# Sequence 0's filter products with frequencies on the partitions

## The chip, the core and the metric

The kernel runs on one core of a Trainium2 chip. The metric is the device time of one execution in microseconds (us), as the median of several runs. The core has five engines with a queue each: PE (TensorE, with its weight loads shown apart as PEld), DVE (VectorE), ACT (ScalarE), POOL (GpSimd) and SP (which here only issues transfers). Transfers run on 16 DMA engines. SBUF holds tiles of up to 128 partitions, PSUM takes what PE makes, and DVE and ACT copy it out.

## What is computed

For each of 8 sequences of 3008 rows and 256 channels, a real Fourier transform along the rows, a product with a complex filter, and the transform back. Then an RMS norm and a gated FFN on each row:

```
X = rfft(x, axis=1)                       # x (8, 3008, 256): 1505 frequencies
y = irfft(X * (filt_r + 1j * filt_i), n=3008, axis=1)
t = y.reshape(24064, 256)
xn = t / sqrt(mean(t * t) + 1e-6) * rms_g
out = (silu(xn @ w_gate) * (xn @ w_val)) @ w_out     # 256 -> 1536 -> 256
```

The filters are two fp32 tables of 1505 x 256, 1.5 MB each. All inputs come in fp32; the matmuls of the kernel run in fp16.

## The kernel before

**The transform.** 3008 is 47 x 64. Stage A transforms along the 64 (matmul with `wa`), which leaves 32 groups `k2` (K2 = 32) of 96 rows (KR = 96: real and imaginary part of 48 values). Stage B is a matmul of each group with its own 96 x 96 table `wb[:, k2]`. Its result are the frequencies, 48 (SL) real and 48 imaginary, of which 24 ascend (k2 + 64 q) and 24 are mirrored (64 j - k2). They are multiplied with the filter. Stage Bi goes back with the tables `wi`, stage Ai with `wai`, and what comes out is `y` in the order that the norm wants.

**The FFN.** For each sequence there are 6 blocks of up to 512 rows, and 12 slices (`jt`) of the hidden width per block. One (sequence, block, slice) is a slot; there are 576. A slot's PE work is four matmuls of 512 columns (`gv`, L501, to `pg` and `pv`), and, two slots later, four of 256 columns (`down`, L526). ACT makes the silu (`sg`), DVE the product with `pv` (`hh`).

**The order.** It is written out by hand (`manual_schedule`). Each engine works its instructions off in the order of the program. While the FFN of one sequence runs, the mixing of the next is laid into its slots: a planner (`at`, `fit`, `a_plan`, `b_plan`, `norm_plan`) places units at slots so that two PSUM banks are not asked for twice and the estimated loads of ACT and DVE stay within a bound. The units are `a_unit` (stage A, one matmul of 512 columns and a copy), `z_store` and `t2_load` (a turn through DRAM), `b_unit` (four matmuls of 96 columns, `psb`), `s_part` and `add_unit` (the complex product with the filter `ff` and its sum), `yt_load` (a DMA transpose), `bi_unit`, `t4_load` (DMA transpose), `n_unit`, `sq_unit`, `stat_unit`, `xt_unit` and `tr_unit` (norm, and DMA transpose to `xn`).

**Sequence 0** has no FFN ahead of it to hide in, so it has a path of its own, the opening, with PE in place of the DMA turns:

1. `x_load` on POOL's queue, then `a0_unit` (L367) with short fills of PE (`fill`, L436).
2. `f_load`: the filter comes in six pieces, with 128 partitions of four whole rows each, on POOL's queue; `wb`, `wi` and two thirds of the FFN's weights (`w_load`) follow there.
3. `f_unit` (L399): the filter is turned by PE to channels on the partitions, and copied by ACT to `ff[128 channels, half, k2, 3 * 48]` (imaginary negated, imaginary, real). `f_neg` (POOL) makes the negated part, `f_last` one row.
4. `tr0_unit` (L377): the data are turned by PE to `t2`, 96 rows on the partitions.
5. For each of 16 units (four k2, one half of the channels): `b_unit` with the data as the stationary operand, so that channels are on the partitions of `psb`; two products on DVE, `s_part` (L238 with the real filter, L241 with the imaginary one and the two parts of `psb` swapped); `yt0_unit` (L428) adds the two and turns them back on PE, to 96 rows on the partitions; `bi_unit` (L292) does stage Bi.
6. `t4_first` (L444), `first_norm` (L456 to L480) for the first block, and `t4_load` by DMA for the others. Four `a_unit`s of sequence 1 and some fills stand between these steps.

Then the slots begin. `seen` (L681) is a tiny POOL copy that reads a transposed tile; what POOL issues after it waits for that tile.

Of the kernel before, what the change touches and what calls it, by code (L numbers as in the profile page):

```python
# [10 lines left out]
FP32 = mybir.dt.float32  # L11
# [27 lines left out]
def _make_tables():  # L39
# [58 lines left out]
    return tab, wb.astype(f), wi.astype(f)  # L98
# [3 lines left out]
def kernel(  # L102
# [13 lines left out]
    tab_np, wb_np, wi_np = _make_tables()  # L116
    tab_d = nc.inline_tensor(tab_np, name="tab_t").ap()
    wb_d = nc.inline_tensor(wb_np, name="wb_t").ap()
    wi_d = nc.inline_tensor(wi_np, name="wi_t").ap()

# [10 lines left out]
    sqp = ctx.enter_context(tc.tile_pool(name="sqp", bufs=2))  # L131
# [3 lines left out]
    hp = ctx.enter_context(tc.tile_pool(name="hp", bufs=4))  # L135
# [10 lines left out]
    wb = glob.tile([P, K2, KR], FP16)  # L146
# [4 lines left out]
    ff = glob.tile([P, 2, K2 + 1, 3 * SL], FP32)  # L151
# [37 lines left out]
    def bank(i, name):  # L189
        pool, tag = ((psM, "mx"), (psG, "pg"), (psV, "pv"), (psB, "mb"), (psO, "po0"))[i]  # L190
        return pool.tile([P, 512], FP32, tag=tag, name=name)
# [51 lines left out]
    def b_unit(b, i, bk=3, e=0):  # L243
        g, dh = divmod(i, 2)
        ps = bank(bk, "psb")[:, 0:4 * KR]
        for k in range(4):
            kk = 4 * g + k
            nc.tensor.matmul(ps[:, ts(k, KR)], st[b]["t2"][kk // KC][:, kk % KC, ds(dh * P, P)],  # L248
                             wb[0:KR, kk, :], start=True, stop=True)
# [4 lines left out]
    def b_soft(b, i, v=None):  # L254
        g, dh = divmod(i, 2)
        ps = bank(3, "psb")[:, 0:4 * KR]
        for k in range(4):
            kk = 4 * g + k
            nc.tensor.matmul(ps[:, ts(k, KR)], st[b]["t2"][kk // KC][:, kk % KC, ds(dh * P, P)],
                             wb[0:KR, kk, :], start=True, stop=True)  # L260
# [111 lines left out]
    def tr0_unit(g, eng):  # L372
        pool, tag = ((psO, "po0"), (psO, "po1"), (psM, "mx"))[g % 3]
# [9 lines left out]
    fst = {}  # L383
    FR4 = 4

    def f_load(i, f):
        if i not in fst:
            fst[i] = stg.tile([P, 2, FR4, D], FP32, tag="stg", name="fs")
        t = fst[i]
        row = FR4 * P * i if i < 2 else NF - 1 - FR4 * P  # L390
        for src in ((filt_i, filt_r)[f],):
            nc.gpsimd.dma_start(t[:, f].rearrange("p a d -> p (a d)"),
                                raw(src, row, [[FR4 * D, P], [1, FR4 * D]]))

    def f_unit(i, f, dh, e):
        t = fst[i]
        ps = bank(1 + "AV".index(e), "psf").rearrange("p (a q) -> p a q", a=FR4)
        for a in range(FR4):
            nc.tensor.transpose(ps[:, a, :], t[:, f, a, ds(dh * P, P)], idf)  # L399
        v = ps.rearrange("p a (q s) -> p s a q", s=16)  # L400
        fk = ff[:, dh, 0:K2].rearrange("p (t k) c -> p t k c", k=4)
        fu = ff[:, dh, 1:K2 + 1].rearrange("p (t k) c -> p t k c", k=4)[:, ::-1, ::-1, :]
        lo = SL * (1 + f) + 8 * i
        hi = lo + H
        if i < 2:
            copy(e, fk[:, :, :, lo:lo + 8], v[:, 0:8])
            copy(e, fu[:, :, :, hi:hi + 8], v[:, 8:16])
        else:
            copy(e, fk[:, :, :, lo:lo + 8], v[:, 8:16])
            copy(e, fu[:, :, :, hi:hi + 7], v[:, 0:8, :, 1:8])  # L410

    def f_last():
        v = ff.rearrange("p e k (s q) -> p e k s q", s=3)
        for dh in range(2):
            nc.gpsimd.tensor_copy(out=v[:, dh, 0, 1:3, H:SL - 1], in_=v[:, dh, K2, 1:3, H:SL - 1])
# [5 lines left out]

    def yt0_unit(i, eng, bk, ks=slice(0, 4)):
        g, dh = divmod(i, 2)
        s = st[0]["s"][i][1]
        ps = bank(bk, "psy")[0:KR].rearrange("p (k t) -> p k t", k=4)
        for k in range(4)[ks]:
            for e in range(2):
                nc.tensor.matmul(ps[:, k, :], s[e][:, k, :], ident, start=(e == 0), stop=(e == 1))  # L428
        if g not in st[0]["yt"]:
            yt_tile(0, g)  # L430
        copy(eng, st[0]["yt"][g][0:KR, ks, dh, :], ps[:, ks])
# [146 lines left out]
    with tc.manual_schedule():  # L578
# [49 lines left out]
        for u in todo[0:2]:  # L628
            f_unit(*u, "A")
# [240 lines left out]
```

## Time and profile before

| | |
|---|---|
| median of 3 runs | 859.22 us (858.91 to 859.23) |
| profiled execution | 859.02 us |
| its span | 857.2 us |
| PE, DVE, ACT, POOL busy in the span | 849.3, 556.1, 612.8, 300.4 us |
| first FFN matmul (`pg`, L501) in the chain of waits | 43.28 us |
| 16-unit product stage, DVE | 21.54 to 36.97 us |
| DMA moved | 108.24 MB |

The profile is of one execution of the program. Starts are counted from the start of the span. A line number can be that of a helper (`copy` is L195 on ACT and L197 on DVE). The span does not hold all of the execution's time: 1.8 us lie around it. PE records overlap, so a single matmul's duration is longer than its distance to the next.

### The profile page before, as it was taken

Reading aid. Unit: us, or ns where it says so; the run is one execution under the profiler, and the core shown is the slowest. Engines: PE = TensorE matmul, PEld = TensorE weight load, DVE = VectorE, ACT = ScalarE, POOL = GpSimd, SP = SyncE. Lnnn points to the kernel's source line nnn. Section 1 sums busy time; section 2 is a strip of 40 time slices with the busy share of each in tenths; the row PEclk is TensorE's granted clock in tenths of the full one; section 3 lists DMA queues with packets and bytes.
Section 4 is the critical chain, followed back from the end, with each engine's and each line's share of the span. In section 5 each row is a group of like instructions: output and inputs, shape, how many; then the busy total and the mean of one; then the engine's idle time right before and its main releaser. Section 6 shows DMA issues by size and latency. Waiting matters only on the chain.

```text
span 857.2 us, 16980 instructions
## 1 busy us (share of the span) xinstructions
PE 849.3 (99%) x6117; PEld 531.9 (62%) x6117; DVE 556.1 (65%) x922; ACT 612.8 (71%) x1343; POOL 300.4 (35%) x349
## 2 busy tenths in 40 slices
PE   8999999999999999999999999999999999999997
PEld 6756666666656666666666666666666666665654
DVE  5857655776666666666666676767666665555554
ACT  4986878786687757887578865887567765777444
POOL 5725732543154413443144430444123430132000
PEclk9999999999999999999999999999999999999999
DMA  9997698756976566747746648534554331521101
GB/s 284 271 182 151 148 191 162 148 124 143 186 137 133 117 134 119 158 113 129 157 126 110 130 99 172 119 77 117 129 115 93 99 72 41 125 52 50 63 25 50
DMA packets 199293, 108.24 MB, mean 126 GB/s; under 512 B 159622, under 2 KB 183576, under 8 KB 199208
## 3 DMA queue, kind: packets, MB, share of 16 engines
q1 hardware_dynamic: 190520, 85.78, 44.2%
q0 software_dynamic: 8544, 21.24, 12.8%
q8 instruction: 48, 0.79, 0.4%
q14 instruction: 37, 0.30, 0.1%
q10 hardware_dynamic: 144, 0.13, 0.0%
HBM read 45.78 MB, written 35.65 MB: 95 GB/s over the span
## 4 chain that ended last, share of the span: by engine, by line
PE 97%; DMA 1%; DVE 0%; ACT 0%; POOL 0%; issue 0%; POOLq 0%
PE po L526 29%; PE pv L501 28%; PE pg L501 28%; PE psb L248 3%; PE psi L292 3%; PE psn L321 2%; PE psa L204 2%; DMA fs<-in_filt_i_dram 1%; PE psy L428 1%; PE psf L399 1%; PE pst L377 0%; POOL xc L186 0%; DVE s L238 0%; ACT ff L195 0%; ACT sq L458 0%
## 5 line engine op out<-in xcount | busy, mean ns | idle before, releaser
L506 DVE TENSOR_TENSOR hh<-pv,sg 128x512 f16<-128x512 f32 (+1 forms) x577 | 391.5, 679 | 284.0 <-ACT sg L505 219.9
L505 ACT ACTIVATE sg<-pg 128x512 f16<-128x512 f32 (+1 forms) x577 | 337.5, 585 | 214.5 <-PE pg L501 210.7
L501 PE MATMUL pg<-xn,wg 128*128 128x512 f16 (+2 forms) x1156 | 337.9, 374 | 0.0
L501 PE MATMUL pv<-xn,wv 128*128 128x512 f16 (+2 forms) x1156 | 337.8, 374 | 0.0
L526 PE MATMUL po<-wo,hh 128*128 128x256 f16 x2256 | 332.6, 272 | 0.0
L526 PEld LDWEIGHTS <-hh 128*128 128x128 f16 x2256 | 213.5, 98 | 105.5
L275 POOL TENSOR_TENSOR ss<-s,s 128x384 f16<-128x384 f16 x112 | 101.9, 911 | 267.1 <-DVE s L241 239.5
L501 PEld LDWEIGHTS <-wv 128*128 128x128 f16 x1156 | 113.0, 98 | 130.6 <-issue 0.2
L501 PEld LDWEIGHTS <-wg 128*128 128x128 f16 x1156 | 111.6, 98 | 16.8 <-issue 0.2
L347 POOL TENSOR_TENSOR xt<-y,rho 128x1024 f16<-128x1024 f32 (+1 forms) x47 | 87.3, 1858 | 2.9
L329 ACT ACTIVATE junk<-y 128x256 f16<-128x256 f32 x184 | 76.0, 413 | 2.9
L241 DVE TENSOR_TENSOR s<-psb,ff 128x384 f16<-128x384 f32 x124 | 67.6, 547 | 0.3 <-POOL ff L419 0.3
L238 DVE TENSOR_TENSOR s<-psb,ff 128x384 f16<-128x384 f32 x124 | 67.6, 547 | 0.3 <-ACT ff L195 0.2
L195 ACT ACTIVATE uu<-psi 128x384 f16<-128x384 f32 (+1 forms) x127 | 61.8, 487 | 1.0
L195 ACT ACTIVATE y<-psn 128x512 f32<-128x512 f32 (+1 forms) x95 | 55.8, 588 | 4.4 <-PE psn L321 0.2
L292 PEld LDWEIGHTS <-yt 96*128 96x128 f16 x512 | 35.5, 97 | 26.2 <-issue 0.2
L339 POOL TENSOR_TENSOR rho<-u,mhalf 128x4 f32<-128x4 f32 (+1 forms) x47 | 47.6, 1012 | 3.9
L337 POOL TENSOR_SCALAR u<-ss 128x4 f32<-128x4 f32 (+1 forms) x47 | 9.1, 194 | 106.4 <-ACT junk L329 105.2
L292 PE MATMUL psi<-wi,yt 96*128 96x96 f16 x512 | 42.9, 205 | 0.0
L195 ACT ACTIVATE t<-psa 128x512 f16<-128x512 f32 x69 | 40.9, 594 | 2.4 <-PE psa L204 0.9
L248 PE MATMUL psb<-wb,t 96*128 96x96 f16 x480 | 40.0, 206 | 0.0
L248 PEld LDWEIGHTS <-t 96*128 96x128 f16 x480 | 29.3, 97 | 10.7 <-issue 0.2
(91 smaller groups left out, 361.0 us busy)
## 6 DMA issues: line engine op xcount, KB each, us to landing
out_dram<-o SPq DMA_DIRECT2D x40, 512.0 KB, 3.6
xc<-in_x_dram POOLq DMA_DIRECT2D x31, 384.0 KB, 5.7
z_tmp<-t SPq DMA_DIRECT2D x28, 384.0 KB, 2.6
t<-z_tmp SPq DMA_DIRECT2D x28, 384.0 KB, 6.0
out_dram<-o SPq DMA_DIRECT2D x7, 384.0 KB, 3.1
fs<-in_filt_i_dram POOLq DMA_DIRECT2D x3, 512.0 KB, 10.7
fs<-in_filt_r_dram POOLq DMA_DIRECT2D x3, 512.0 KB, 11.3
ws<-in_moe_w_gate_dram POOLq DMA_DIRECT2D x3, 512.0 KB, 10.0
```

What stands on the lines that cost most here:

```text
L195: nc.scalar.activation(out=out, in_=in_, func=AXT.Copy, **({} if scale is None else {"scale": scale}))
L238: eng.tensor_tensor(out=o, in0=ps, in1=f1, op=ALU.mult)
L241: eng.tensor_tensor(out=o, in0=ps[:, :, ::-1, :], in1=f2, op=ALU.mult)
L248: nc.tensor.matmul(ps[:, ts(k, KR)], st[b]["t2"][kk // KC][:, kk % KC, ds(dh * P, P)], wb[0:KR, kk, :], start=True, stop=True)
L275: nc.gpsimd.tensor_tensor(out=ss3[g % 3][:, :, dh, 0:KR], in0=s[0], in1=s[1], op=ALU.add)
L292: nc.tensor.matmul(ps[:, k, :], yt[0:KR, k, dh, :], wi[0:KR, 4 * g + k, :], start=True, stop=True)
L329: nc.scalar.activation(out=junk, in_=y[:, i, ts(u, D)], func=AXT.Square, accum_out=ss[:, 2 * i + u:2 * i + u + 1])
L347: nc.gpsimd.tensor_tensor(out=xt[:, 0:n, :], in0=y.rearrange("p a (u d) -> p (a u) d", u=2)[:, 0:n, :], in1=rho[:, 0:n].unsqueeze(2).to_br ...
L501: nc.tensor.matmul(ps[:, (r0 - q0) * P:(r1 - q0) * P], wt[:, dt_, ts(jt, P)], xn[:, r0:r1, dt_, :], start=(dt_ == 0), stop=(dt_ == 1))
L505: nc.scalar.activation(out=sg[:, c], in_=pg[:, 0:w], func=AXT.Silu)
L506: nc.vector.tensor_tensor(out=hh[:, c], in0=pv[:, 0:w], in1=sg[:, c], op=ALU.mult)
L526: nc.tensor.matmul(po[q - 1][:, 0, :] if own else po[q // 2][:, q % 2, :], hh_of[(b, m, j)][:, ts(q, P)], wo[:, j, :], start=(j == 0 and ( ...
```

## The change

For sequence 0 alone, the frequencies stay on the partitions through the products:

- The filter is loaded unturned: `fs[c]` holds, for eight k2, 48 rows of the imaginary filter and 48 of the real one on 96 partitions, ascending rows in runs of 8 KB, mirrored rows in runs of 1 KB. A row without a frequency gets zeros from a small table. Loads of `wb`, filter and a new table `w2` go chunk by chunk through SP's queue, behind a one-element memset of `wb` on DVE.
- `b0_unit` makes, for two k2 and all 256 channels, two matmuls each: with the table's columns as they are (imaginary, real) and shifted by 48 (real, imaginary). For that `wb` has 144 columns. `w2` holds the two tables of stage Bi that go with the two products.
- The product of each with `fs` is on DVE, or, for ten of the 16 first products (`soft`), a copy on ACT and the product on POOL.
- `bi0_unit` adds the two products within stage Bi (eight matmuls in place of four); `yt0_unit` and its copies go.
- `ff` is still made for the sequences 1 to 7, in 16 units `f_unit(g, dh)` of four k2: seven in the gaps from the end of the opening through the first slot, nine in the slots 6 to 19, and `f_neg` in the slots 1 and 21.
- `w_load` stages the FFN's gate and value weights in the space of `ff`, on SP's queue; the third is loaded between the `t4_load`s. `wo_load`, `x_load(1, ...)`, `w_gain` and `wi` come at other places. All twelve `a_unit`s of sequence 1 are in the slots, before eight were.
- `sqp` has 1 buffer (2 before), `hp` 3 (4 before).

```diff
+    wi = wi[:KR]
+    w2 = np.stack([np.concatenate([-wi[:SL], wi[:SL]]), np.concatenate([wi[SL:], wi[SL:]])], axis=1)
...
-    sqp = ctx.enter_context(tc.tile_pool(name="sqp", bufs=2))
+    sqp = ctx.enter_context(tc.tile_pool(name="sqp", bufs=1))
-    hp = ctx.enter_context(tc.tile_pool(name="hp", bufs=4))
+    hp = ctx.enter_context(tc.tile_pool(name="hp", bufs=3))
...
+    def f_load(c, zeros):
...
+        for h, src in enumerate((filt_i, filt_r)):
+            q0 = h * SL
+            for lo, n in ((0, 16), (16, 8)):
+                nc.sync.dma_start(t[q0 + lo:q0 + lo + n].rearrange("p k d -> p (k d)"),
+                                  raw(src, 64 * lo + k0, [[64 * D, n], [1, KC * D]]))
+            q0 += H
...
+            for lo, n in ((0, 16), (16, 7)):
+                nc.sync.dma_start(t[q0 + lo:q0 + lo + n, z:KC, :],
+                                  raw(src, 64 * (lo + 1) - k0 - z, [[64 * D, n], [-D, KC - z], [1, D]]))
...
+    def f_mm(g, dh, bk):
+        ps = bank(bk, "psf")[:, 0:4 * KR].rearrange("p (k q) -> p k q", k=4)
+        c, r = divmod(g, 2)
+        for k in range(4):
+            nc.tensor.transpose(ps[:, k, :], fs[c][0:KR, 4 * r + k, ds(dh * P, P)], idf[0:KR, 0:KR])
+        return ps
...
+    def b0_unit(u, soft):
+        ps = [(psG, psV)[e].tile([P, 512], FP32, tag=("pg", "pv")[e], name="psb")[0:KR] for e in range(2)]
+        c, r = divmod(2 * u, KC)
+        for e in (1, 0):
+            for k in range(2):
+                nc.tensor.matmul(ps[e][:, ts(k, D)], wb[0:KR, 2 * u + k, ds((1 - e) * SL, KR)], st[0]["t2"][c][:, r + k, :], start=True, stop=True)
...
+        for e in (1, 0):
+            o = s[:, ts(e, 512)]
+            if soft and e == 1:
+                v = xtp.tile([P, 4, D], FP16, tag="xt", name="psc").rearrange("p a d -> p (a d)").bitcast(FP32)[0:KR]
+                nc.scalar.activation(out=v, in_=ps[e], func=AXT.Copy)
+                nc.gpsimd.tensor_tensor(out=o, in0=v, in1=f, op=ALU.mult)
+            else:
+                nc.vector.tensor_tensor(out=o, in0=ps[e], in1=f, op=ALU.mult)
+
+    def bi0_mm(i, ks, ps):
+        g, dh = divmod(i, 2)
+        for k in range(4)[ks]:
+            kk = 4 * g + k
+            for e in range(2):
+                nc.tensor.matmul(ps[:, k, :], s0[kk // 2][:, e, kk % 2, ds(dh * P, P)],
+                                 w2s[kk // KC][:, e, kk % KC, :], start=(e == 0), stop=(e == 1))
...
     def first_norm():
...
+        f_unit(2, 0, "V", 3)
+        f_unit(3, 0, "V", 1)
         copy("V", y[:, 0, :], psn[0])
...
-            fill(1)
...
         copy("A", y[:, 1, :], psn[1])
+        late = [(0, 1, "V", f_mm(0, 1, 2)), (1, 1, "V", f_mm(1, 1, 3)), (2, 1, "A", f_mm(2, 1, 0))]
...
+        nc.vector.memset(wb[0:1, 0, 0:1], 0.0)
+        for c in range(NC):
+            w2_tile(c)
+            nc.sync.dma_start(wb[0:KR, ts(c, KC), :], wb_d[:, ts(c, KC), :])
+            f_load(c, False)
+            w2_load(c)
+        w_load(0)
+        w_load(1)
...
+        for g in range(4):
+            tr0_unit(g, "VAVA"[g])
+        for u in range(UN):
+            b0_unit(u, u % 3 > 0)
+            if u < 3:
+                tr0_unit(4 + u, "AVA"[u])
+            if u == 2:
+                tr0_unit(7, "A")
+            if u >= 4:
+                bi0_unit(u - 4)
+        w_gain(0)
+        wo_load(0)
+        x_load(1, 0)
+        w_gain(1)
+        bi0_unit(UN - 4)
+        bi0_unit(UN - 3)
+        early_f = [(0, 0, "V", f_mm(0, 0, 1)), (1, 0, "A", f_mm(1, 0, 2))]
...
+        for cs in (slice(0, 4), slice(4, H)):
+            for dh in range(2):
+                bi0_out(UN - 2 + dh, "VA"[dh], psl[dh], cs)
...
+        for u in early_f:
+            f_out(*u)
         t4_first()
-        a_unit(1, 1, "V", 0)
-        fill(1, 3)
-        for c in range(NXC):
+        for c in range(2):
             t4_load(0, c)
+        w_load(2)
+        for c in range(2, NXC):
+            t4_load(0, c)
+        nc.sync.dma_start(wi[0:KR], wi_d)
         nc.gpsimd.tensor_copy(out=seen, in_=st[0]["t4"][1][:, 0, 0:4])
+        x_load(1, 1)
+        wo_load(1)
+        x_load(1, 2)
+        ahead = first_norm()
+        w_gain(2)
+        x_load(1, 3)
         wo_load(2)
...
-            for i in range(4 * (b == 1), 12):
+            for i in range(12):
...
+            at(fit(6 if n == 0 else 11 + n, *need), f_unit, g, dh, e, 0 if k == "M" else 3)
+        at(1, f_neg, 0, 12)
+        at(21, f_neg, 12, 20)
...
-                z = a_plan(b, [i for i in range(12)])
+                z = a_plan(b, [2 + 5 * i // 6 for i in range(12)])
```

## The prediction

> **What bounds the kernel now.** I read the page's busy shares first, then the chain of waits over the first 80 us, then the windows by stage.
>
> ```profile
> PE 849.3 (99%) x6117; PEld 531.9 (62%) x6117; DVE 556.1 (65%) x922; ACT 612.8 (71%) x1343; POOL 300.4 (35%) x349
> ```
>
> PE has work in 99% of the span, so after the opening the time is a sum of PE work. Something can be won only where PE does work that could vanish or waits: the opening, sequence 0's mixing.
>
> ```profile
> 3.63 9.21 DMA fs<-in_filt_i_dram
> ...
> 12.98 1.07 PE psf L399 x8
> ...
> 23.25 0.57 DVE s L238
> ...
> 36.50 0.47 DVE s L241
> ...
> 40.34 1.09 ACT sq L458 x2
> ...
> 43.28 0.22 PE pg L501 x2
> ```
>
> These are pieces of the chain (start, length). Until 12.98 it is the filter's load, until 23.25 filter turning (psf) mixed with turning the data back (pst), until 36.97 the products. There PE's psb, psy and psi and DVE's 32 products keep one beat, 0.93 us for each of 16 units. Then come 6.31 us of small steps until the first FFN product at 43.28.
>
> ```profile
> 0.00:13.00 13.00, 10.81 (x75) 5.73 (x75) 5.34 (x15) 4.82 (x8) 7.14 (x16) 1.00 0.88 202
> 13.00:23.30 10.30, 9.94 (x124) 9.42 (x124) 7.40 (x13) 7.06 (x24) 5.50 (x10) 1.00 1.03 409
> 23.30:37.00 13.70, 13.04 (x225) 11.73 (x225) 13.61 (x29) 12.75 (x29) 13.37 (x23) 1.00 1.13 301
> 37.00:43.30 6.30, 5.94 (x58) 3.57 (x59) 4.27 (x10) 5.53 (x13) 2.33 (x5) 1.00 1.12 150
> 43.30:60.40 17.10, 17.10 (x103) 9.88 (x102) 9.49 (x15) 14.94 (x32) 5.51 (x8) 1.00 0.90 190
> ```
>
> Columns: window, its length, busy time of PE, PEld, DVE, ACT, POOL, granted clock, DMA share, GB/s. DVE is full in the product stage (13.61 of 13.70). From 43.3 PE is full and DMA still 0.90 busy, which matters below. The clock is 1.00 throughout.
>
> **The base.** The profiled execution took 859.02 us: 857.2 of span and 1.8 around it. The median of the runs is 859.22. The sum below is a difference, and I put it on the median.
>
> **When the new stage can start.** The x loads keep their place. A memset of one element of `wb` is put on DVE behind the copies of the third a0 unit, which end at 9.70, and SP's loads of wb, filter and w2 wait for it. SP's queue does nothing else here. SP's small DMAs took 0.23 to 0.40 us each to issue (tab, tail). Thirteen of them (wb and twelve filter pieces) at 0.3 put the last piece of chunk 0 at 13.5; tab landed 2.2 us after its issue; so products start near 15.8. tr0_unit's four turnings (0.45 us of PE each, L377) are done by then. Before, the first product that mattered for the end started at 23.25.
>
> **The stage.** The filter's turning leaves the opening but for seven units in its gaps, and yt0_unit goes (16 x 0.45 us of PE, 16 x 0.59 of ACT). A unit is now four products of 256 columns: L501's of that shape come 0.11 apart, 0.43 a unit, 6.9 for 16. bi0_unit has eight matmuls where L292's four took 0.17: 0.34, 5.5 for 16. With the eight turnings (3.6) PE needs 16.0 us, of which about 13 lie between 15.8 and the last product. DVE has 22 products of 512 elements. Two such instructions (L506) took 1.29, one 0.69, so 0.60 apart: 13.2, and one turning copy of 0.65: 13.9. GpSimd has ten products: 128x384 with two f32 inputs took 1.00 (L238 on POOL), so 512 take 1.00 to 1.33; I take 1.30, nearest to proportional: 13.0, beginning with the second unit. ACT copies ten (0.50 apart), evacuates some 12 bi0 units (0.44) and three turnings (about 1.0): 13.3. So four engines need 13 to 14 us each, in order, with two banks per product. DVE alone gives 15.8 + 13.9 = 29.7; I add 0.9 for hand-offs among four nearly full engines (bounds 0 and 2.5): last product at 30.6, against 36.97.
>
> **From the last product to the first FFN product.** Before 6.31. Now: sums of the last halves 0.35, the first rows' copy 0.2, the rest of the rows and a filter copy ahead of the turned copy on DVE and ACT 0.45 + 0.46, that copy 0.6: psn starts 2.1 us after the last product (before 3.07). From psn to the first pg it was 3.24; two filter copies (0.47 each) now stand ahead of the copy of y on DVE, and three filter units (0.38 each) ahead of psr on PE. The wait for Square and Sqrt hides most; I charge 0.45. So 2.1 + 3.7 = 5.8 (5.3 to 6.8), and the first pg is at 36.4, 6.9 us earlier.
>
> **What moves into the loop.** PE is full there, so this is paid whole. Four a_units of sequence 1 that filled gaps of the opening: 4 x 0.216 = 0.87. Nine filter units: four f32 turnings of 128 columns took 0.44 (L399); with 96 columns 0.33 if columns count, 0.44 if the weight load does. I take 0.38: 3.4 (3.0 to 4.0). Together 4.3. Their nine evacuations, mostly on ACT in slots 15 to 19, go beside a window with ACT at 13.44 of 17.60: 0.2 charged, up to 1.0. `junk` has one buffer, but only ACT writes it; sg with three of four buffers is filled two slots ahead at most; both at nothing, 0.2 per slot at worst while ACT is full. w_gain(0) needs w_load(0), 1 MB behind 5.1 MB on SP; at 409 GB/s it is in by 27, before GpSimd finishes its products, so `wg` is ready by 33.
>
> **Sum.** -6.9 + 4.3 + 0.2 = -2.4: 859.2 - 2.4 = **856.8**. The parts' bounds alone make it 855 to 860.
>
> **Rival 1, slower: the loads miss the first block.** What was loaded by 39 (wi, all weights, two thirds of wo, three x chunks) is now partly loaded during the loop. GpSimd's order after the t4 loads is `seen`, x(1,1), wo(1), x(1,2), w_gain(2), x(1,3), wo(2), f_neg, then the statistics and xt for block 1; SP has w_load(2) between the t4 loads, and wi behind them.
>
> ```profile
> 39.00 8.08 SPq L306 DMA_TRANSPOSE t<-uu  x4
> ...
> 54.22 1.23 SPq L356 DMA_TRANSPOSE xn<-xt  x1
> ```
> ```profile
> 45.89 0.19 POOL L681 COPY seen<-t 128x4 f16<-128x4 f16 x1 [6.56 <-DMA t<-uu]
> ...
> 57.33 0.19 POOL L361 COPY seen<-xn 128x4 f16<-128x4 f16 x1 [3.13 <-DMA xn<-xt]
> ```
>
> The first lines are SP's, the others POOL's (start, length, idle before). `seen` came 6.9 us after the first t4 issue. With uu complete at 31.8 it comes at 38.7; wo(0) and x(1,0), issued near 33.5, share the DMA engines and can add 3 us. From there to the turned xn of block 1 I count x and wo issues 2.1, w_gain(2) 4 x 0.67 = 2.7, two more issues 1.45, f_neg 2 x 0.67, statistics 1.3, xt 1.9, transpose 3.1: 13.9, so 52.6 to 55.7. Slot 12 began 17.1 us after the first pg; with 1.2 us of added PE work (four a_units, one filter unit) it wants xn at 54.7. So between 2.1 to spare and 1.0 late. The stock of bytes looks worse: before, DMA was busy almost without pause to 54, when x(1,3) landed; now 1.2 MB more is moved (w2 added, the tables cut to 96 rows), 3 us at 400 GB/s, less 2.5 us of pauses: 54.5, where slot 10 wants it at 36.4 + 14.1 + 1.0 = 51.5. That is 3 us late, and wo(2) behind it; 4.5 with the transposes queued behind: 856.8 + 4.5 = **861.3**. It decides from about 4 us of waiting in slots 4 to 12. Against it: only x(1,3) and wo(2) must be in by slot 10, and t4's last two, wi and z may come later. Chance 0.33.
>
> **Rival 2, no change: the filter's arrival paces the products.** Half of each chunk is read in runs of 1 KB, in pieces of 8 and 7 rows. Loads of 384 KB landed in 6.0 us with 512 B runs (t<-z_tmp) and 2.6 with 3 KB runs written (z_tmp<-t): up to 3.4 us for the short runs, perhaps half with 1 KB; four chunks with about 385 KB of them would be up to 6.8 us. The last chunk is wanted at 26.3 and, at 409 GB/s for 5.1 MB from 9.85 with 2.2 to land, comes at 24.6. If 1 KB runs or half-used engines cost 3.4 us, it comes at 28.0 and the end moves 1.7: **858.5**. The same follows if a GpSimd product takes 1.5 us instead of 1.3. Chance 0.25.
>
> The Trainium skill, DMA: Bandwidth & Descriptors, section "Why a DMA increments its semaphore by 16 and not by 1", speaks for this rival: a DMA uses only as many of the 16 engines as divides its slowest dimension, on SP's queue the lowest-numbered ones. By it the 8-row and 7-row pieces all fall on the same half of the engines, which carry 98 KB of each chunk; at 409/16 GB/s that is 3.8 us a chunk, 15.3 in all instead of 12.6, and I estimate 1 to 1.5 us on the end. No row of before shows a load of so few long rows, so I leave it in the chance.
>
> **How the numbers follow.** A measurement of this kernel can tell about 0.2%, 1.7 us, from no change. The forecast (856.8; 854.5 to 857.5) has 0.42 and counts as faster, rival 2 0.25 as same, rival 1 0.33 as slower. For 8 in 10 the range reaches from 853.8 (no hand-off losses, filter units at 0.33) to 862.6 (both rivals in part).
>
> **What would show it.** Right: s0 products from about 15.8 to 30.6 without waits for `fs`; first pg at 36.4; nine psf groups of 0.38 us among the FFN products; PE without idle time from there; `psy` gone. Wrong: PE or PEld idle in slots 4 to 12, with wo, xc, xn or wg named as releaser (rival 1); DVE and POOL waiting for `fs` between chunks (rival 2); a first pg after 39, which would leave nothing.

## The result, and the profile after

The changed kernel takes **889.8 us** (median of 4 runs, 888.0 to 892.5) against 859.1 us of the kernel before on the same chip: a ratio of 1.0361, 95% interval 1.0333 to 1.0388. It is 31 us slower, where 856.8 was forecast. The profiled execution is the longest of the four, 892.49 us, with a span of 890.7, so 33.5 us more than the span before. All starts below are of profiled executions.

From the page, PE's busy time and the clock in 40 slices of 22.3 us:

```profile
PE 860.4 (97%) x6060; PEld 542.4 (61%) x6060; DVE 554.6 (62%) x913; ACT 612.1 (69%) x1327; POOL 301.9 (34%) x338
...
PEclk9659999999999999999999999999999999999999
```

Fewer matmuls (6060 instead of 6117), but 11 us more of busy time: in the second and third slice the granted clock was 0.6 and 0.5. PE is also without work for 30 us of the span; before it was 8.

The chain of waits (start, length):

```profile
12.15 5.73 DMA fs<-in_filt_i_dram
...
22.24 9.10 DMA fs<-in_filt_r_dram
...
31.36 8.80 DMA fs<-in_filt_i_dram
...
40.17 8.20 DMA fs<-in_filt_i_dram
...
48.39 4.83 DMA ff<-in_moe_w_gate_dram
...
53.85 0.69 DVE s L455
...
62.67 0.86 PE psn L506 x5
...
69.06 0.58 PE pg L556 x2
...
78.51 10.93 DMA z_tmp<-t
```

From 12 to 53 the opening is nothing but the load of the filter. (The piece that starts at 48.39 is named after a load of weights that follows the filter on SP's queue. The product behind it, L455, reads the filter and not these weights, so I take it for the wait for the last filter pieces.) Before, that part of the chain ended at 12.84. The four chunks let DVE go on at 21.97, 33.39, 44.13 and 53.25, some 10.4 us apart. The last product ends at 58.0 (36.96 before), the first FFN product starts at 69.06 (43.28 before).

The windows (columns as in the prediction: PE, PEld, DVE, ACT, POOL, granted clock, DMA share, GB/s):

```profile
13.00:24.00 11.00, 6.60 (x80) 5.64 (x79) 4.74 (x9) 5.11 (x7) 2.00 (x2) 0.95 0.76 148
...
24.00:32.00 8.00, 4.35 (x46) 3.99 (x44) 2.33 (x4) 3.85 (x6) 0.50 (x1) 0.86 1.06 116
32.00:40.00 8.00, 5.87 (x47) 5.34 (x47) 3.17 (x5) 2.65 (x5) 3.76 (x3) 0.57 0.75 117
40.00:48.00 8.00, 3.59 (x28) 3.15 (x27) 3.17 (x5) 2.53 (x5) 3.21 (x3) 0.50 0.83 127
...
60.00:69.00 9.00, 8.12 (x64) 6.93 (x63) 4.04 (x11) 5.15 (x11) 2.92 (x6) 0.50 1.19 194
...
78.50:90.00 11.50, 9.06 (x54) 5.12 (x53) 4.63 (x7) 6.67 (x12) 2.29 (x2) 1.00 1.16 214
```

Read the last two columns together. From 24 to 48 the DMA engines are busy for a share of 0.75 to 1.06, but they move 116 to 127 GB/s; before the change it was 409 at a share of 1.03 (13.00 to 23.30). A full share is not a full rate: the packets themselves take longer. No compute engine is full; DVE, which had 13.61 of 13.70 us before, has 3.17 of 8. The clock is 0.50 right through the steps that lead to the first FFN product, where PE is busy. And from 78.5 to 90 PE is idle for 2.4 us with the DMA share still over 1; the chain spends that time in a store of sequence 1's first stage to `z_tmp`, which takes 10.93 us from its issue. The first such store took 7.9 before the change.

SP's lines and POOL's `seen`, as before:

```profile
61.88 3.48 SPq L311 DMA_TRANSPOSE t<-uu  x2
...
80.90 2.81 SPq L361 DMA_TRANSPOSE xn<-xt  x1
```
```profile
68.82 0.19 POOL L713 COPY seen<-t 128x4 f16<-128x4 f16 x1 [6.08 <-DMA t<-uu]
...
90.53 0.19 POOL L366 COPY seen<-xn 128x4 f16<-128x4 f16 x1 [9.66 <-DMA xn<-xt]
```

`seen` comes 6.9 us after the first transpose, as before (6.9) and as forecast; but xn of block 1 takes 9.6 us from its issue instead of 3.1.

**Where the 33.5 us of span are.** 25.8 until the first FFN product. From there to the silu of slot 12 (the first of block 1) 22.4 us instead of 17.6: 4.8. From slot 12 to slot 36 38.2 instead of 35.4: 2.8, about what eight filter units take (0.33 each). Behind slot 36 nothing (761.0 in both). These add up to 33.4, the rest is rounding. Of the 4.8, 2.6 are idle time of PE (19.77 us of 22.38 busy) and 1.2 the work of four `a_unit`s and one filter unit; the rest is not traced.

### The profile page after: what moved, and what is told of

Its sections match the earlier page's. It is cut to its first block, busy times and chain, and to the rows that moved or that the text cites. A ratio compares the mean times of both kernels' runs of the same rounds, so it can differ in the third digit from the quotient of the medians.

```text
span 890.7 us, 16918 instructions
## 1 busy us (share of the span) xinstructions
PE 860.4 (97%) x6060; PEld 542.4 (61%) x6060; DVE 554.6 (62%) x913; ACT 612.1 (69%) x1327; POOL 301.9 (34%) x338
## 4 chain that ended last, share of the span: by engine, by line
PE 91%; DMA 7%; DVE 1%; SPq 1%; issue 0%; ACT 0%; POOL 0%; DVEq 0%; ACTq 0%; POOLq 0%
PE po L581 27%; PE pg L556 27%; PE pv L556 27%; DMA fs<-in_filt_i_dram 3%; PE psn L326 2%; PE psi L297 2%; PE psb L253 2%; PE psa L209 2%; DMA z_tmp<-t 1%; DMA fs<-in_filt_r_dram 1%; DMA xc<-in_x_dram 1%; DMA t<-uu 1%; DMA ff<-in_moe_w_gate_dram 1%; PE psf L430 0%; PE psi L462 0%
## 5 line engine op out<-in xcount | busy, mean ns | idle before, releaser
L200 ACT ACTIVATE uu<-psi 128x384 f16<-128x384 f32 (+1 forms) x128 | 62.2, 486 | 24.1 <-PE psi L462 23.0
L246 DVE TENSOR_TENSOR s<-psb,ff 128x384 f16<-128x384 f32 x108 | 59.2, 548 | 0.0
L243 DVE TENSOR_TENSOR s<-psb,ff 128x384 f16<-128x384 f32 x108 | 59.2, 548 | 0.0
L297 PEld LDWEIGHTS <-yt 96*128 96x128 f16 x448 | 31.6, 97 | 25.9
L297 PE MATMUL psi<-wi,yt 96*128 96x96 f16 x448 | 37.5, 205 | 0.0
L253 PE MATMUL psb<-wb,t 96*128 96x96 f16 x432 | 36.1, 206 | 0.0
L326 PE MATMUL psn<-t,tab 128*128 128x512 f16 x94 | 35.2, 374 | 0.0
```

What stands on the lines that cost most here:

```text
L200: nc.scalar.activation(out=out, in_=in_, func=AXT.Copy, **({} if scale is None else {"scale": scale}))
L243: eng.tensor_tensor(out=o, in0=ps, in1=f1, op=ALU.mult)
L246: eng.tensor_tensor(out=o, in0=ps[:, :, ::-1, :], in1=f2, op=ALU.mult)
L297: nc.tensor.matmul(ps[:, k, :], yt[0:KR, k, dh, :], wi[0:KR, 4 * g + k, :], start=True, stop=True)
```

## The experiments

Fourteen kernels, each timed beside the kernel before. The table has the first FFN product, the silu of slot 12 (`sg`; 17.6 us behind the first product before) and the span, all from the profiled execution, then the median with its ratio.

| kernel | first pg | slot 12 | span | time us | ratio (95%) |
|---|---|---|---|---|---|
| before | 43.28 | 60.8 | 857.2 | 859.1 | |
| changed | 69.06 | 91.4 | 890.7 | 889.81 | 1.0361 (1.0333 to 1.0388) |
| e1_wide | 45.4 | 72.1 | 873.0 | 876.17 | 1.0198 (1.0177 to 1.0218) |
| e2_wide_1kb | 45.0 | 72.3 | 871.3 | 874.44 | 1.0178 (1.0157 to 1.0198) |
| e3_8kb_runs | 62.2 | 84.8 | 883.6 | 885.33 | 1.0304 (1.0284 to 1.0325) |
| e4_step4 | 62.4 | 88.6 | 889.4 | 890.74 | 1.0351 (1.0325 to 1.0377) |
| e5_warm | 63.8 | 90.7 | 889.9 | 892.16 | 1.0388 (1.0373 to 1.0404) |
| e6_zeros | 63.8 | 84.4 | 883.6 | 886.12 | 1.0312 (1.0296 to 1.0327) |
| e7_split | 51.1 | 80.0 | 879.1 | 881.30 | 1.0265 (1.0248 to 1.0283) |
| e8_order | 51.7 | 73.1 | 874.4 | 876.46 | 1.0201 (1.0185 to 1.0216) |
| e9_128 | 42.6 | 75.7 | 878.6 | 877.37 | 1.0201 (1.0183 to 1.0218) |
| e10_order_warm | 46.2 | 73.3 | 874.5 | 875.61 | 1.0191 (1.0176 to 1.0206) |
| e13_resident | 38.2 | 66.0 | 865.5 | 867.27 | 1.0096 (1.0081 to 1.0112) |
| e15_resident_early | 43.5 | 62.5 | 862.5 | 864.28 | 1.0060 (1.0046 to 1.0073) |
| e18_resident_gated | 39.0 | 61.5 | 860.5 | 863.31 | 1.0046 (1.0033 to 1.0058) |
| e19_128_mid | 48.4 | 70.2 | 869.6 | 872.46 | 1.0158 (1.0142 to 1.0173) |

Slot 12 on ACT, before and in the changed kernel:

```profile
60.84 0.60 ACT L505 ACTIVATE sg<-pg 128x512 f16<-128x512 f32 x1 [0.27 <-PE pg L501]
```
```profile
91.44 0.62 ACT L560 ACTIVATE sg<-pg 128x512 f16<-128x512 f32 x1
```

The span follows slot 12, not the first FFN product: span minus slot 12 is 796.4 before and 799 to 803 in all the others. That is the key to the second half of the study. (The expectations of e15, e18 and e19 took the silu of slot 13 for that of slot 12: their 28.6, 18.3, 19.8 and 34 us behind slot 0 are 26.8, 16.7, 17.9 and 32.1 us for slot 12.)

### Why the filter comes so late

**e1_wide**, each chunk as one load over all 96 partitions:

```diff
-        for h, src in enumerate((filt_i, filt_r)):
...
+        nc.sync.dma_start(t[0:KR].rearrange("p k d -> p (k d)"), raw(filt_i, k0, [[15 * D, KR], [1, KC * D]]))
```

> The filter's 8 to 12 pieces of a chunk become one load of the same 96 rows of 8 KB, on all 96 partitions (other rows of the filter, so the product part computes with wrong filter values). In the changed kernel the chunks were complete at about 22, 33, 44 and 53 us, some 10 us apart. All three theories (A: a piece that lands on 8 or 16 neighbouring partitions is slow; B: SP waits for earlier transfers to land before it issues the next, and there are too many of them; C: the runs of 1 KB are slow) expect a chunk in 3 to 4 us, the last at 24 to 28 us, the last product near 31 and the first pg near 38. What remains above 859 us is then not the filter's arrival: my sum of the prediction gives 857 to 860, the late loads of the first block up to 865.

**e2_wide_1kb**, the same in eight loads of 1 KB per partition:

```diff
+        for k in range(KC):
+            nc.sync.dma_start(t[0:KR, k, :], raw(filt_i, k0 + k, [[15 * D, KR], [1, D]]))
```

> As many transfers per chunk as pieces (8), each on all 96 partitions with one run of 1 KB per partition, the same bytes (other rows of the filter). A (few partitions) expects a chunk in 3 to 5 us and a time within 4 us of the one wide load. B (number of transfers on SP) expects about 10 us a chunk as in the changed kernel, 885 to 892 us. C (1 KB runs) expects it slower than the changed kernel, since all runs are now of 1 KB where half were: over 892.

**e3_8kb_runs**, the narrow pieces kept, the mirrored halves in 8 KB runs too:

```diff
-                nc.sync.dma_start(t[q0 + lo:q0 + lo + n, z:KC, :],
-                                  raw(src, 64 * (lo + 1) - k0 - z, [[64 * D, n], [-D, KC - z], [1, D]]))
+                    nc.sync.dma_start(t[q0 + lo:q0 + lo + n].rearrange("p k d -> p (k d)"),
+                                      raw(src, 64 * lo + 32 * part + k0, [[64 * D, n], [1, KC * D]]))
```

> The pieces stay on their 16, 8 or 7 neighbouring partitions, but the mirrored halves are read in ascending runs of 8 KB too (other rows of the filter); in chunk 0 two transfers fewer. A expects no gain beyond 3 us: about 10 us a chunk, 885 to 892. B expects the same. C expects chunks in 5 us and 870 or less.

Measured: with wide loads DVE's chunks are 5.2 us apart (e1) and 4.5 (e2) instead of 10.4, and the first FFN product comes 24 us earlier, in runs of 8 KB (e1) as in runs of 1 KB with eight times as many transfers (e2). That is still less than all three theories expected of e1 (a chunk in 3 to 4 us, at most 865 us). e3 wins 4.5 us of time, which is more than the 3 that A allowed: its chunks are 8.3 us apart, so in the narrow pieces the short runs cost something as well. But neither the length of the runs nor the number of transfers was the main cause; what is left is that each transfer goes to 7 to 16 neighbouring partitions. The packets say the same: from 24 to 53 one of 8192 bytes took some 430 to 1470 ns in the changed kernel (median 773), about 510 in e1; one of 1024 bytes 120 in the median and up to some 250, against 46 in e2. The rate in e1:

```profile
18.00:24.00 6.00, 5.17 (x70) 4.91 (x69) 4.86 (x8) 4.96 (x7) 2.50 (x2) 1.00 1.05 265
```

Better than 116, yet far from 409, at a full share. **e9_128** asks whether the 96 partitions are the reason:

```diff
-        nc.sync.dma_start(t[0:KR].rearrange("p k d -> p (k d)"), raw(filt_i, k0, [[15 * D, KR], [1, KC * D]]))
+        nc.sync.dma_start(t.rearrange("p k d -> p (k d)"), raw(filt_i, k0, [[11 * D, P], [1, KC * D]]))
```

> e1_wide with 128 instead of 96 partitions in every chunk load: wb 288 KB, filter 1024 KB (rows 11 apart, so other values), w2 384 KB, 1.70 MB a chunk instead of 1.27. Theory (the rate depends on how evenly the transfer covers the partitions): before the change 128-partition loads went at 409 GB/s, in e1_wide 96 partitions at some 250; then 1.70 MB a chunk take 4.2 to 4.6 us, less than e1_wide's 5.1 although they are a third more bytes; the last chunk is complete at 31 to 33 us (34.59 there), 8192-byte packets near 320 to 350 ns (520 there). Rival (SP's queue or the mix with the products' stage caps it at 250 GB/s): 6.8 us a chunk, last chunk near 40, slower than e1_wide.

```profile
20.00:30.00 10.00, 8.78 (x119) 7.89 (x117) 8.63 (x15) 9.06 (x18) 8.08 (x7) 1.00 1.01 412
...
42.00:78.00 36.00, 23.52 (x130) 12.97 (x129) 13.89 (x22) 17.33 (x37) 11.48 (x17) 0.91 1.17 187
```

412 GB/s on the same queue, 8192-byte packets at 309 ns, a third more bytes in less time, and a first FFN product at 42.6. So the rate goes by how the partitions are covered. Pieces of 7 to 16 neighbours give 116 to 127 GB/s, 96 partitions 249 to 265 (e1, 18 to 36), 128 give 412. The Trainium skill has the rule: SBUF — State Buffer, section "Door 1: The DMA port swizzle (why `[64,N]` ≈ `[32,N]`)", says that the bandwidth of a DMA depends on how many of 16 ports its partitions reach, and gives 104 GB/s for partitions 0 to 15 and 328 to 436 for all 128. The 116 to 127 and the 412 lie near it. For 96 partitions the Trainium skill has no figure there; by its map two thirds of the rows fall on half of the ports, from which I estimate 309 GB/s if all ports together carry 412; 249 to 265 were measured. The second line of the fence is the surprise of this run: from 42 to 78, which holds the way from the first FFN product (42.6) to slot 12 (75.7), PE is busy for only 23.5 of 36 us, and with the filter in time the kernel is still at 877.4. That is taken up below.

**e4_step4** keeps the reference's filter and spreads each piece's rows over every fourth partition, with permuted tables:

```diff
+        tv = t[0:KR].rearrange("(q g) k d -> g q k d", g=4)
...
+                nc.sync.dma_start(tg[lo:lo + n].rearrange("p k d -> p (k d)"),
                                   raw(src, 64 * lo + k0, [[64 * D, n], [1, KC * D]]))
```

> The same pieces with the same runs, but each piece's rows are put four partitions apart (row q of group g on partition 4q + g), so that a 16-row piece spans 61 partitions instead of 16; the tables of stage B for sequence 0 and w2 are permuted to fit, stage B's two tables are loaded into the space of wb and wi, and wb is loaded again later (0.3 MB more ahead of the products, 0.6 MB more behind them). A expects a chunk in 4 to 5 us, the last at 27 to 30 us, and 860 to 868. B and C expect no change: 10 us a chunk, 888 to 892.

SP's queue in the changed kernel (two unspread pieces), then in e4:

```profile
21.13 0.70 SPq L413 DMA_DIRECT2D fs<-in_filt_i_dram  x2
```
```profile
22.77 1.31 SPq L410 DMA_DIRECT2D fs<-in_filt_i_dram  x2
24.12 1.49 SPq L419 DMA_DIRECT2D fs<-in_filt_i_dram  x2
```
```profile
12.00:46.00 34.00, 22.61 (x230) 19.84 (x231) 14.00 (x23) 16.41 (x28) 10.03 (x8) 0.80 0.58 163
```

The expectation of a gain missed. The transfers are quicker now (packets of 1024 bytes at 46 ns and of 8192 at 472 in the median, DMA share 0.58), though the pieces are the same. But SP takes 0.51 to 0.87 us to issue one (median 0.65), where an unspread piece took 0.28 to 0.43 (0.32), and it issues without a pause to 46.0. Theory B, the issuing, which e2 had ruled out for wide loads, is the bound here. **e7_split** is e4 with the real filter's pieces on GpSimd's queue and the zero rows written by GpSimd (the edit is against e4):

```diff
-                nc.sync.dma_start(tg[lo:lo + n].rearrange("p k d -> p (k d)"),
+                (nc.sync, nc.gpsimd)[h].dma_start(tg[lo:lo + n].rearrange("p k d -> p (k d)"),
```

> e4_step4 (pieces whose rows go to every fourth partition) with the pieces of the real part issued on GpSimd's queue and those of the imaginary part left on SP's, and the zero rows written by GpSimd. Theory (with spread partitions the filter's arrival is bound by the time of issuing on one queue): the 44 transfers that SP issued from 12.0 to 45.9 us become some 26 on SP and 18 on GpSimd, side by side, and the last chunk is complete at 28 to 31 us, the last product at 32 to 34 and the first FFN product at 39 to 42 (62.44 in e4_step4, 43.28 before the change). The time then shows what the first block's waits are worth: 862 to 866 us if they are 0 to 3 us, 868 to 874 if they are as large as in e1_wide (8 us) or larger. Rival (the DMA engines cannot take these pieces faster, however they are issued): chunks stay 7 us apart, first FFN product after 55, time above 880. If issuing on GpSimd costs more than 1 us each, the chunks are paced by that queue (last chunk near 35).

The first FFN product comes 11.4 us earlier than in e4, at 51.1, not at 39 to 42. From 20 to 30 the DMA share is 0.97 at 200 GB/s and packets are slow again (4096 bytes in 270 ns, 159 before the change). With both queues at work the DMA engines are full again, as in e1; that the cover of the 96 partitions is what fills them here too is not shown.

**e6_zeros** replaces the eight one-partition loads of zeros:

```diff
-                nc.sync.dma_start(t[(h + 1) * SL - 1:(h + 1) * SL, z:KC, :].rearrange("p k d -> p (k d)"),
-                                  zero_d[h:h + 1, 0:(KC - z) * D])
+            nc.gpsimd.memset(t[0:KR].rearrange("p k d -> p (k d)"), 0.0)
```

> The changed kernel, with the zero rows of the four filter tiles written by four GpSimd memsets of 96 partitions instead of eight one-partition loads of 8 KB on SP ahead of x; nothing else differs. Theory: those eight loads hold single DMA engines and are why x landed 1.6 to 1.9 us later than before the change; without them the second a0 unit comes near 7.6 us, the memset that releases the filter's loads near 9.6 (11.22 with them), every chunk and the first FFN product some 1.6 us earlier, and the time is 887.5 to 888.5 us. Rival: x is late for another reason (the two tiles' other early work), the memset stays at 11 us and the time within 0.6 us of 889.8.

The memset that releases the filter comes at 9.82 instead of 11.22, so the loads of zeros had delayed x by 1.4 us, as the theory said. The time falls by 3.7 us, more than it said, because the chunks are also only 9.2 us apart (20.33, 31.27, 40.24, 47.95; 10.4 in the changed kernel). Why those loads, long landed, slow the later ones, no run shows.

### What the half clock costs

**e5_warm** keeps PE at work while it waits for chunks:

```diff
         for u in range(UN):
+            if u in (6, 10, 14):
+                fill({6: 26, 10: 19, 14: 17}[u], 0)
             b0_unit(u, u % 3 > 0)
```

> The changed kernel with 26, 19 and 17 idle products (each 128x512, result unused) on TensorE ahead of units 6, 10 and 14 of the sequence-0 products, that is in TensorE's waits for the filter; nothing else differs. Theory (granted clock): in the changed kernel the clock is 0.50 from about 30 to 69 us because TensorE waits, and this doubles the PE steps from the last filter product to the first FFN product (11.05 us there, 7.1 in e1_wide, where it fell less) and the bi0 units behind each chunk. Then with the clock held up the last product comes at most 1 us earlier (the chunks still arrive 10.4 us apart), the first FFN product 4 to 6 us earlier (63 to 65 instead of 69.06), and the time is 884 to 886 us. Rival (the tail waits for loads and small steps, not for the clock): the clock reads 1.0 in the windows from 40 to 69, but the first FFN product stays within 1.5 us of 69 and the time at 888 to 891 us.

```profile
60.00:69.00 9.00, 6.49 (x59) 4.51 (x57) 6.00 (x13) 5.76 (x12) 3.25 (x6) 1.00 1.08 170
```

The clock is up (0.50 in the same window of the changed kernel), the steps from the last product to the first FFN product take 6.7 us instead of 11.0, the first FFN product comes 5.2 us earlier, and the time does not fall (892.2). Both theories were half right: the clock is what stretched the tail, and it costs next to nothing, because slot 12 comes at 90.7 instead of 91.4. Something else sets it.

### What sets slot 12

**e8_order** is e1 with the later loads put ahead:

```diff
+        w_load(2)
...
+        wo_load(0)
+        x_load(1, 0)
+        x_load(1, 1)
+        wo_load(1)
+        x_load(1, 2)
         w_gain(0)
```

> e1_wide (each filter chunk as one load of 96 whole partitions, other filter rows, so other values) with the later loads put earlier: the last third of the gate and value weights behind the second third on SP, ahead of the transposes of sequence 0, and on GpSimd's queue wo(1) and the x loads of sequence 1 ahead of the weight scaling, not behind `seen`. Theory (the first block's 8 us of waits in e1_wide come from the order of the queues): the waits for w_gain, wo, xc and xn in slots 2 to 12 shrink to 0 to 3 us, slot 12 begins 19 to 22 us after the first FFN product (26.1 in e1_wide), and the time is 868 to 872 us. Rival (the DMA engines are full from the filter to slot 12, so that order only moves the wait): the transposes of sequence 0 or the block's xn land later by what the loads gain, slot 12 stays 25 to 28 us behind, the time 874 to 879 us.

**e10_order_warm** is e8 with `fill(8, 0)` ahead of units 6, 10 and 14.

> e8_order with 8 idle products (128x512, unused) on TensorE ahead of units 6, 10 and 14. In e8_order the first block's waits fell to 1.8 us but the time did not, because the clock was 0.50 from about 36 to 52 us and the steps from the last product (40.23) to the first FFN product (51.68) took 11.4 us, against 7.1 in e1_wide. Theory (so the gain of the order was given back by the clock): with the clock held up the tail is 7 to 8 us, the first FFN product at 46 to 48.5, slot 12 still 21 to 23 us behind it, and the time 870 to 873 us. Rival (the end of the first block is set by when the loads are through, as e5_warm suggests, where a first FFN product 5.2 us earlier gained nothing): waits return in slots 2 to 12 by what the first product gains, time 875 to 878.

```profile
PE psn L326 <- DMA t<-uu: 5.6, 1, 5.6
```

This line is from PE's waits in e10 (in all, times, longest). In e8 the waits for wo and xc were gone (slot 12 follows the first FFN product by 21.4 us, as the theory said, against 26.7 in e1), but the tail fell into the half clock (0.50 from 40 to 52). e10 cured that, and the 5.5 us at the first FFN product came back as a wait for the transposes of sequence 0. Slot 12 stays at 73.1 and 73.3, in e1 it was 72.1. By the time, the rivals of both were right: placed straight behind the filter, the loads only trade places with the transposes.

**e13_resident** takes the filter away: one chunk is loaded (as one load of 96 partitions), and used for all four. With it go six of the eight loads of zeros.

```diff
     def f_load(c, zeros):
+        if c:
+            fs[c] = fs[0]
+            return
```

> The changed kernel with only chunk 0 of the filter loaded (one load of 96 partitions) and its tile used for all four chunks, so that other values come out; wb, w2, the queues' order, all products and all filter units as in the changed kernel. 2.3 MB fewer are loaded and no product waits for a filter chunk. It tests the rest of the forecast's sum. Forecast's steps: products from 15 to 17 us, last product 30 to 32, first FFN product 36 to 38.5, no waits in the first block (the missing bytes are 5.6 us of loading at 409 GB/s), time 855.5 to 859. Rival (the stage's hand-offs, the tail or the loop's added work were too low too): last product after 33 or tail above 6.8, time 860 to 864. Rival 1 of the forecast (the first block's loads come too late even so): first FFN product before 38.5, but 3 us or more of waits for wo, xc, t or xn in slots 2 to 12, time 860 to 864.

```profile
28.00:34.00 6.00, 5.21 (x82) 4.54 (x79) 4.38 (x9) 4.76 (x12) 6.00 (x7) 1.00 0.01 5
```
```profile
25.36 6.21 POOL L443 TENSOR_TENSOR s<-psc,fs 96x512 f16<-96x512 f32 x5
...
34.20 0.84 POOL L612 DMA_DIRECT2D wo<-in_moe_w_out_dram  x1
35.03 0.61 POOL L191 DMA_DIRECT2D xc<-in_x_dram  x1
...
44.60 0.19 POOL L703 COPY seen<-t 128x4 f16<-128x4 f16 x1 [6.04 <-DMA t<-uu]
44.84 0.59 POOL L191 DMA_DIRECT2D xc<-in_x_dram  x1
```

Products from 16.62 to 31.06 without a pause, first FFN product at 38.2: the stage is as forecast. But slot 12 is at 66.0, 27.8 us behind, and the time is 867.3. The last reading of the expectation holds in kind: rival 1, here without three quarters of the filter. Its 860 to 864 us were too low. Of the 9.0 us over 17.6 and 1.2 for the moved units, 4.9 are idle time of PE; after the waits the clock reads 0.88 from 38.2 to 66. The window shows why: from 28 to 34 the DMA engines move 5 GB/s. The loads of sequence 1 and of `wo` stand on GpSimd's queue behind its ten products and the weights' scaling, while before the change they were issued from 26.1 to 31.1. When they start, the transposes start too (35.03 on SP).

**e15_resident_early** issues them ahead of the products (and the last third of the weights behind the second on SP), **e18_resident_gated** when chunk 0 is in, with one small copy in front (its filter values are those of e13):

```diff
+        nc.gpsimd.tensor_copy(out=seen[0:KR], in_=fs[0][0:KR, 0, 0:4])    # e18 only
+        for c in range(3):
+            x_load(1, c)
+        for c in range(2):
+            wo_load(c)
         UN = K2 // 2
```

> e13_resident (one filter chunk loaded and used for all four, other values) with the later loads in the DMA engines' free stretch: x(1,0..2), wo(0) and wo(1) issued on GpSimd ahead of its ten products instead of behind them, the last third of the gate and value weights on SP behind the second third. In e13_resident the DMA share was 0.03 from 28 to 31 us and 0.00 from 31 to 34, because these loads stood behind GpSimd's last product (31.5); then they met the transposes of sequence 0, and the first block lost about 9 us (sg of slot 12 came 28.6 us after that of slot 0, 18.3 before the change, 1.2 of it added work). Theory (the order of GpSimd's queue, not the number of bytes, makes those waits): slot 12 comes 19.5 to 22 us behind slot 0, the first FFN product within 1 us of 38, and the time is 857 to 860.5 us. Rival (the transposes, the stores to z_tmp and xn need this long themselves): slot 12 still 26 us or more behind, time 864 to 868. Third possibility: the early loads take the engines from wb and w2, and the products wait for w2 or psi for it: first FFN product after 40, time 860 to 864.

> e15_resident_early with one small GpSimd copy from the filter's tile ahead of the early loads of x(1,0..2), wo(0) and wo(1), so that they start when chunk 0 is in and not before it. In e15_resident_early the first block had no waits (slot 12 came 19.8 us behind slot 0), but those loads delayed chunk 0 (first product at 20.84 instead of 16.62) and the first FFN product came at 43.5, as before the change, and the time was 5.2 us over before: that is the price of the work moved into the loop. Theory (with the filter's arrival, the waits and the early loads out of the way, what is left is a first FFN product about 5 us earlier and 5 us of moved work): first product near 17, GpSimd 1 to 2 us behind, first FFN product at 38.5 to 40.5, slot 12 19.5 to 21 us behind slot 0, time 859 to 861.5 us, so no gain even with one chunk of filter. Forecast's sum (moved work 4.5, tail 5.8): 857 to 858.5. Rival (the early loads slow wb and w2 or GpSimd's products more than that): first FFN product after 41, time over 861.5.

The windows of e15, then PE's longest wait in e18:

```profile
44.00:64.00 20.00, 20.00 (x123) 11.78 (x121) 12.45 (x21) 16.35 (x34) 9.51 (x14) 1.00 0.95 205
```
```profile
PE po L571 <- DMA wo<-in_moe_w_out_dram: 1.9, 1, 1.9
```

In e15 PE has no idle time in the first block, and slot 12 follows the first FFN product by 18.9 us, about 17.6 and the moved 1.2. But the loads hold up chunk 0 (first product at 20.84), the third possibility of its expectation, so that the first FFN product is 5.3 us later than in e13. Slot 12 itself comes 3.5 us earlier: at least that much of the 9.0 is the place of those loads in GpSimd's queue, and the rest of the waiting is covered by the later start. In e18 the first FFN product is at 39.0, three waits of the block remain (2.9 us, 1.9 of it for `wo`), slot 12 is at 61.5, 4.5 us earlier than in e13, the time 863.3 (861.5 to 864.6): outside the forecast's 857 to 858.5, and above the 859 to 861.5 of the theory by about those waits.

**e19_128_mid** does this for e9, where all four chunks come at 412 GB/s (values as in e9): the five loads are issued after unit 9.

> e9_128 (all filter chunks as 128-partition loads at 412 GB/s, other values, 1.70 MB a chunk) with the last third of the weights behind the second on SP and x(1,0..2), wo(0) and wo(1) issued on GpSimd after unit 9 of the products instead of behind all of them. In e9_128 the first FFN product came at 42.6, before that of the kernel before, yet slot 12 came 34 us behind slot 0, 14.5 of it waits, and the time was 877.4. Theory (order of the queues): GpSimd loses 3.3 us to the five issues, the first FFN product comes at 43 to 46, slot 12 20 to 25 us behind slot 0, time 864 to 870 us. Rival (with all bytes moved the engines are full until slot 12, so that order only moves the waits, as e8_order and e10_order_warm gained nothing): slot 12 more than 27 us behind, time 872 to 878.

Measured is between the two: slot 12 follows 21.8 us behind the first FFN product instead of 33.1, but that comes at 48.4 instead of 42.6, as GpSimd's last products are late and the clock drops (0.50 from 40 to 50). The net is 4.9 us. So order gives back part. That the bytes keep the rest, since with the whole filter to load there is no free stretch to put the loads into, is my reading (411 GB/s from 20 to 30, 307 from 30 to 40); no run shows it apart.

## Why the prediction was wrong, point by point

**The step that failed** is in rival 2: "The last chunk is wanted at 26.3 and, at 409 GB/s for 5.1 MB from 9.85 with 2.2 to land, comes at 24.6." It let DVE go on at 53.25. The 409 GB/s were read from a window in which all transfers covered 128 partitions, and were applied to pieces of 7 to 16 neighbouring ones, of which the trace before had no row. Measured was 116 to 127 GB/s. With wide loads it was 249 to 265 on 96 partitions (e1) and 412 on 128 (e9), and from e1 to e9 little but the cover changes. Rival 2 had the right kind and sign of effect (products waiting for `fs` between chunks, as "what would show it" named), but its bound, 3.4 us, came from run lengths. These are worth nothing in wide loads (e2); in the narrow pieces they are worth 6.9 us (in e3 DVE goes on with the last chunk at 46.35 instead of 53.25), of the 28.6 between 24.6 and 53.25. The 1 to 1.5 us estimated by the Trainium skill's rule on the number of engines (DMA: Bandwidth & Descriptors, section "Why a DMA increments its semaphore by 16 and not by 1") are as far off; the pieces' slowness is that of neighbouring partitions (e4: same pieces, spread, quicker).

**Start of the products.** 15.8 forecast, 16.62 in e13 (with two of the eight loads of zeros); 21.97 in the changed kernel. Of the difference 1.4 us are the loads of zeros ahead of x, which I had not charged.

**The stage.** 14.8 us with hand-offs were forecast, 14.4 measured in e13. GpSimd's product took 1.25 instead of 1.30, DVE's were 0.60 to 0.62 apart. Right.

**Last product to first FFN product.** 5.8 forecast (5.3 to 6.8). 7.1 in e13 at full clock, over the bound, and 11.0 in the changed kernel at half clock. The drop of the clock was not foreseen, since the forecast had no long waits of PE; it turned out to be nearly hidden (e5).

**Moved work.** 4.5 with the evacuations. The filter units are 0.33 us each in the slots (the lower of the two readings), so nine and four `a_unit`s make 3.8. In e15 nothing waits in the first block, the first FFN product is 0.2 later than before, and the span is 5.3 longer: 5.1 in all. From the first product to slot 36 it is 57.2 us instead of 53.0: 4.2. The last 0.9 lie behind slot 36, and are not traced.

**The sum, with the filter and the waits out of the way.** From e13's first FFN product and e15's moved work: -5.1 + 5.1 = 0, not -2.4. So by this sum the planned gain was not there even without the transfers' fault; no run shows both at once. e18, the nearest to that, is 1.0046 (1.0033 to 1.0058) of the time before.

**Rival 1** was right in mechanism: order of GpSimd's queue, loads of x and `wo` meeting the transposes, `xn` of block 1 late. Its size was 4.5 us, with slot 12 17.6 + 1.2 + 4.5 = 23.3 us behind the first FFN product. Measured is 27.8 in e13, though 2.3 MB less are moved, and 33.1 in e9. I had counted single loads one after the other and not that the transposes, the stores to z_tmp and these loads go on side by side and each take longer: xn of block 1 took 9.3 us in e13 instead of 3.1, and the store to z_tmp took 13.54 us there and 10.93 in the changed kernel, instead of 7.9. In the changed kernel slot 12 is 22.4 us behind, so 3.6 over 17.6 + 1.2.

## What to carry to other kernels

Before a load is cut into pieces, ask which partitions each piece covers, and price it from a row with the same cover; a DMA share of 1.0 says that the engines are taken, and only the GB/s beside it say what they deliver. When a stage is made shorter, list the loads that used to pass beneath it: here a 5 us earlier first FFN product (e13) met a queue of loads that had not become shorter, and slot 12 came 5 us later than before the change. Find the point that the span really follows (here slot 12, not the first FFN product) before crediting a gain ahead of it.

## What the runs showed of the hardware that was not expected

- Packets of 8192 bytes took 309 ns in loads of 128 partitions (e9), about 510 in loads of 96 (e1), and 430 to 1470 in pieces of 8 and 16 neighbouring partitions (changed kernel, 24 to 53).
- Pieces to every fourth partition kept the DMA engines less busy (share 0.58, e4), but the issue of one on SP took 0.65 us in the median instead of 0.32.
- PE's granted clock read 0.57 and 0.50 from 32 to 48, while it waited for chunks, and 0.50 from 60 to 69, in which PE was busy for 8.1 of 9 us. The Trainium skill, TensorE: Matmul & The Clock Gate, section "HAM oscillation — how this bites in real kernels", describes this for waits on DMA that are longer than its window of 3.4 us; PE's waits for the last three chunks were 5.8, 4.4 and 3.9 us, so the trace agrees. With fills in the waits the clock read 1.00 from 60 to 69 (e5).
- Eight loads of 8 KB to one partition each, issued ahead of x, delayed x by 1.4 us and were worth 3.7 us of time (e6).
